# Two middle pairs of the second sweep: output products with the weights standing, turned, stored to scratch rows and added to the output by whole-chunk transfers

## The chip, the cores and the metric

The kernel runs on one core of one Trainium2 chip. The metric is the device time of one execution in microseconds (us). The engines are named as in the profile: PE is TensorE's matmul, PEld its weight load, DVE is VectorE, ACT is ScalarE, POOL is GpSimd and SP is SyncE, which here only issues DMAs.

## What is computed

Attention between 512 tokens and 32 state rows (8 batches, 8 heads of 64) gives 8 chunks of 544 rows by 512 columns. Two feed-forward blocks follow, over all 4352 rows. The second of them is the one that matters here:

```
x = relu(x @ w_in); x = (x * x) @ w_out            # 512 -> 2048 -> 512
a = x @ w1; b = x @ w2                              # 512 -> 1024, twice
h = (a * b) @ w3                                    # 1024 -> 1024
out = h @ w_out2                                    # 1024 -> 512
```

## The kernel before

The kernel first computes w34 = w3 @ w_out2 (1024 by 512), so that the last block is out = (a*b) @ w34. All products are done in float32 halves: each operand is split into a high and a low part (`split`: a cast on ACT, a difference on DVE), and each product is three matmuls (`PASSES`).

The last block makes two **sweeps** (`s`) over the rows. Sweep 0 takes the first 512 of the 1024 inner features, sweep 1 the others. The 512 token rows of the chunks are taken in **pairs** of chunks (the 32 state rows of all chunks are done apart, in `ab9` and `out9`): sweep 0 takes the pairs (3,4), (5,6), (7,2), (0,1), and sweep 1 the same backwards: (0,1) is its first pair, (7,2) and (5,6) are its middle pairs, (3,4) its last. For each pair:

- `quad` runs four times (m = 0 to 3) and makes a*b for 128 features at a time, with a scheme that needs seven products where eight blocks are multiplied. Its pieces (q0, q1) become the operands z of the next step (`to_z`, `late_z`).
- `out_pair` multiplies them by w34, again with seven products (`product`), and combines them into four blocks "11", "12", "21" and "22" (256 columns of one chunk each). `keep` copies a bank to SBUF, `put` adds a bank to what was kept.
- `make_pair` makes the operands of the next pair from what `load_pair` loads; its parts (`jobs`) are run by `do` between the products.

There are two forms of a product in `out_pair`. In the **straight** form z stands in the array and 256 columns of w34 move: 24 matmuls of 128x256 (line 1531), and rows of the bank are tokens. In the **turned** form w34 stands and 512 columns of z move: 12 matmuls of 128x512 (line 1520), and rows of the bank are output features. A turned block is kept, turned by DVE in 32x32 squares during the next pair's `quad`, and stored in runs of 256 bytes (`turn_out`: per block two transposes, two DMAs on SP's queue and two on POOL's). Before the change the first three pairs of sweep 0 are turned, and all of sweep 1 is straight.

Sweep 0 stores its results to `out`, except the halves of its first pair, which it stores to scratch (`o_scr`). In sweep 1 the first three pairs add theirs to `out` by accumulating DMAs of 256 KB on POOL's queue (line 1573, eight for a pair). The last pair (`ends`) loads sweep 0's halves back (`fetch`, on SP's queue), adds them on DVE and stores the sum.

Two loads of `out_pair` matter for the prediction. The products S3 and S4 take sums of weights from one slot of a tile, and `load_turn(s, 2)` overwrites S4's sum by S3's (two DMAs of 256 KB on SP's queue, line 1459) when the S4 product has read it; the S3 product is the sixth of the seven and can't start before they land. `fetch("12")` and `fetch("21")` are two DMAs of 256 KB each, ahead of them and behind them on the same queue.

Each engine runs its instructions in the order in which a scheduler has put them; `tc.issue_after` keeps one instruction behind another in that order.

Of the kernel before, what the change touches and what calls it, by code (L numbers as in the profile page):

```python
# [8 lines left out]
F32 = mybir.dt.float32  # L9
# [4 lines left out]
ALU = mybir.AluOpType  # L14
# [6 lines left out]
def kernel(  # L21
# [17 lines left out]
    nc = tc.nc  # L39
    B, H, S, D = x.shape  # L40
    NS = state.shape[2]
    DM = H * D
    DF = w_in.shape[1]
    D1 = w1.shape[1]
    T = S + NS
# [9 lines left out]
    NH = DM // 2  # L55
# [18 lines left out]
    dram = ctx.enter_context(tc.tile_pool(name="dram", bufs=1, space=DRAM))  # L74
# [1042 lines left out]
    NH = DM // 2  # L1117
# [193 lines left out]
    def quad(c0, c1, m, behind, in_order, behind_steps, early_jobs=()):  # L1311
        def product(*args, **kwargs):
            with tc.issue_after(left["quad"].ins) if in_order and "quad" in left else nullcontext():
                left["quad"] = product_of(*args, **kwargs)

        def product_of(ps, w, v, first=True, last=True):
            for kt in range(2):
                for k, (wi, vi) in enumerate(PASSES):
                    mm = nc.tensor.matmul(  # L1319
                        ps, W[w, kt][:, wi, m * P:(m + 1) * P], Y[v, kt][:, vi, :],  # L1320
                        start=(first and kt == 0 and k == 0), stop=(last and kt == 1 and k == 2),
                        skip_group_check=True,
                    )
            return mm

        def kept(i, ps):
            t = bp.tile([P, 512], F32, tag=f"s{i}", bufs=1 + (i == 0), name=f"s{i}")
            left["copy"] = nc.scalar.copy(t, ps)  # L1328
            return t

        def plus(t, ps):
            return nc.vector.tensor_tensor(out=t, in0=ps, in1=t, op=ALU.add)  # L1332

        A, D, E, C = bank_m("qa"), bank_y(m % 2, "qd"), bank_y(2, "qe"), bank_y(3, "qc")
        product(A, "A11", "B11", last=False)
        p1 = kept(0, A)
        with tc.issue_after(behind.ins) if behind else nullcontext():
            product(D, "S1", "T1", last=False)
        p5 = kept(1, D)
        with tc.issue_after(behind.ins) if behind else nullcontext():  # L1340
            product(E, "A12", "B21")
        plus(p1, E)
        product(A, "S2", "T2", first=False, last=False)
        u2 = kept(2, A)
        product(D, "S4", "B22", first=False)
        u2_sum = plus(u2, D)
        with tc.issue_after(u2_sum.ins), tc.issue_after(left["copy"].ins):
            for job in early_jobs:
                job()
        product(C, "A22", "T4")  # L1350
        product(A, "S3", "T3", first=False)
        u3 = kept(3, A)
        plus(p5, A)
        q1 = bp.tile([P, 512], F32, tag="qd" if m % 2 else "qb", bufs=1 if m % 2 else 2, name="q1")
        nc.vector.tensor_tensor(out=q1, in0=u2, in1=p5, op=ALU.mult)  # L1355
        if parts and m in behind_steps:
            add_behind(q1[:, :1])
        if m == 0:
            turn_out("11")
        turn_out("21" if m else "12")  # L1360
        plus(u3, C)
        if m % 2:
            q0 = bp.tile([P, 512], F32, tag="qc", bufs=2, name="q0")
        else:
            q0 = pa.tile([P, 512], F32, tag="r", bufs=2, name="q0")
        nc.vector.tensor_tensor(out=q0, in0=p1, in1=u3, op=ALU.mult)
        if m:
            turn_out("22")
        return to_z(m, q0, q1)
# [93 lines left out]
    TURNED = {"11": 5, "12": 6, "21": 2, "22": 4}  # L1463
    to_turn = {}

    def half_of(c, i, kept_back):
        if kept_back:
            o_scr[c, i] = dram.tile([S, NH], F32, name=f"oscr{c}_{i}")
            return o_scr[c, i]
        return out[c * T:c * T + S, i * NH:(i + 1) * NH]  # L1470

    def turn_out(block):
# [7 lines left out]
        for a in range(4):  # L1480
            (nc.gpsimd if a % 2 else nc.sync).dma_start(dst[a], o[a * NS:(a + 1) * NS].rearrange("p k d e -> p k (d e)"))

    TWO = ("s0", "yo", "r", "qb", "qc")

    def place(tag, name):
# [2 lines left out]

    def out_pair(c0, c1, s, jobs, last, first, more):
        ends = s == 1 and not more  # L1490
        turn = s == 0 and more
        jobs, gate, zcast = list(jobs), left["copy"], left["zcast"]
        mms = [left["quad"]]

        def do(n):
            with tc.issue_after(last.ins), tc.issue_after(gate.ins), tc.issue_after(zcast.ins):
                for job in jobs[:n]:
                    job()
            del jobs[:n]
# [8 lines left out]
            return w34_t[u][:, {"A11": 0, "A12": 2, "A22": 3}.get(w, 1)]  # L1508

        def product(*args, **kwargs):  # L1510
            with tc.issue_after(mms[-1].ins) if s == 0 else nullcontext():
                mms.append(product_of(*args, **kwargs))

        def product_of(ps, w, v, first=True, last=True):
# [33 lines left out]
        def keep(block, ps, tp0=0):  # L1548
            ts = []
            for tp, p in enumerate(ps, tp0):  # L1550
                if ends:
                    t = o_in.pop((block, tp))
                    nc.vector.tensor_tensor(out=t, in0=p, in1=t, op=ALU.add)
                else:
                    tag = "tp" if turn and AT[block][tp] == "s1" else AT[block][tp]
                    t = place(tag, "o")
                    nc.scalar.copy(t, p)
                ts.append(t)
            return ts

        def put(block, ts, ps, tp0=0):
            c, i = where(block)
            for tp, t in enumerate(ts, tp0):
                nc.vector.tensor_tensor(out=t, in0=ps[tp - tp0], in1=t, op=ALU.add)  # L1564
                if turn:
                    continue
                rows_t = "(p j) e -> p j e" if c < BLK else "(j p) e -> p j e"
                dst = out[c * T:c * T + S, i * NH:(i + 1) * NH].rearrange(rows_t, j=J)[:, 2 * tp:2 * tp + 2]
                src = t.rearrange("p (j e) -> p j e", j=2)
                if s == 0 or ends:  # L1570
                    nc.sync.dma_start(dst, src)
                else:
                    nc.gpsimd.dma_start(dst, src, accum_op=ALU.add)  # L1573
            if turn:
                to_turn[block] = half_of(c, i, first), ts

        for block in ("11", "22") if ends else ():
            fetch(block)
# [4 lines left out]
        bD = [bank_m("od") for _ in range(2)]  # L1583
        product(bD, "S1", "T1", last=False)
        t22 = keep("22", bD)
        do(1 if turn else 3 if more else 2)
        late(1)
        fetch("12")
        product(bD, "S4", "B22", first=False)
# [80 lines left out]
    for s, todo in enumerate((turns, turns[::-1])):  # L1670
# [16 lines left out]
        for i, (c0, c1) in enumerate(todo):  # L1687
            jobs = []
            for m in range(QM):
                early_jobs = []  # L1690
                if m == QM - 1 and s == 0 and i + 1 < len(todo):
                    jobs = make_pair(raw)
                    early_jobs, jobs = jobs[:2], jobs[2:]
                last = quad(c0, c1, m, after if i == 0 else None, s == 0 and (i > 0 or m > 0), (2,) if i else (0, 2), early_jobs)
                if m == 0 and i + 1 < len(todo):
                    raw = load_pair(*todo[i + 1])
                if m == 1 and i + 1 == len(todo) and s == 0:
                    raw = load_w(1)
# [41 lines left out]
```

## Time and profile before

| | |
|---|---|
| device time, median of 3 runs | 1198.16 us (1197.91 to 1198.72) |
| profiled execution | 1198.95 us, of which the span of the trace is 1196.7 us |
| PE busy | 1185.0 us, 99% of the span |
| DVE, ACT, POOL busy | 948.5, 694.5, 176.1 us |
| DMA | 179.22 MB |
| granted TensorE clock, mean | 0.998 |

The span runs from the first instruction to the end of the last one; some 2.2 us of the profiled execution lie outside it. A matmul's end is modelled, so the rate of PE is read from the starts of consecutive products, not from its busy time.

### The profile page before, as it was taken

The page shows a single profiled execution, that of the slowest core. Times are in us where ns is not written, and L with a number is a line of the kernel's source. Part 1 is how long each engine was busy: PE and PEld are TensorE (multiplying, and loading weights), DVE is VectorE, ACT ScalarE, POOL GpSimd, SP SyncE. Part 2 cuts the span into 40 slices and gives each one's busy share as a digit, 9 for nine tenths or more (in the row PEclk, how much of TensorE's full clock was granted, in tenths as well). Part 3 has the DMA queues.
Part 4 walks back from the last instruction along what each step waited for, and adds up shares of the span by engine and source line. Part 5 has one row for each costly group of instructions (what it writes and reads, how often), then busy time and mean ns, then how long its engine had stood idle before and what let it go on. Part 6 is the DMA issues. An engine that isn't in the chain of part 4 may idle for free.

```text
span 1196.7 us, 18436 instructions
## 1 busy us (share of the span) xinstructions
PE 1185.0 (99%) x6736; PEld 967.4 (81%) x6736; DVE 948.5 (79%) x1697; ACT 694.5 (58%) x1263; POOL 176.1 (15%) x249
## 2 busy tenths in 40 slices
PE   7999999999999999999999999999999999999998
PEld 5677777777777777777888888888888989898988
DVE  6989877778878674677778986989797958787877
ACT  6777556565656565777767663536454525353542
POOL 0000013323331200012231001020100001211210
PEclk9999999999999999999999999999999999999999
DMA  8675778946885933346696685673423631625334
GB/s 253 140 229 191 184 219 224 204 120 177 171 208 166 260 106 110 107 115 111 92 220 230 223 210 133 110 158 76 111 88 98 216 111 33 144 49 127 62 65 139
DMA packets 181876, 179.22 MB, mean 150 GB/s; under 512 B 103433, under 2 KB 134921, under 8 KB 181257
## 3 DMA queue, kind: packets, MB, share of 16 engines
q1 hardware_dynamic: 141128, 109.61, 31.6%
q0 software_dynamic: 38640, 65.03, 25.9%
q10 hardware_dynamic: 2016, 3.41, 0.8%
q8 instruction: 53, 0.87, 0.3%
q14 instruction: 39, 0.31, 0.1%
HBM read 114.43 MB, written 74.06 MB: 158 GB/s over the span
## 4 chain that ended last, share of the span: by engine, by line
PE 96%; DVE 2%; ACT 1%; DMA 1%; issue 0%; SPq 0%; DVEq 0%
PE y L594 22%; PE qa L1319 11%; PE qd L1319 7%; PE ps_w L1132 4%; PE qc L1319 4%; PE qe L1319 4%; PE oa L1531 3%; PE qa L966 3%; PE ps_sw L507 3%; PE od L1531 2%; PE oa L1520 2%; PE ab L1394 2%; PE qd L966 2%; PE y L566 1%; PE od L1520 1%; PE oe L1531 1%
## 5 line engine op out<-in xcount | busy, mean ns | idle before, releaser
L594 PE MATMUL y<-ghl,wo 128*128 128x512 f32 x1152 | 279.7, 392 | 0.1
L594 PEld LDWEIGHTS y<-ghl,wo 128*128 128x128 f32 x1152 | 214.5, 188 | 57.4 <-issue 12.6
L1328 ACT COPY s<-qa 128x512 f32<-128x512 f32 x96 | 56.5, 589 | 173.3 <-PE qa L1319 173.2
L1319 PE MATMUL qa<-yq,wq 128*128 128x512 f32 x576 | 143.3, 389 | 0.0
L538 DVE TENSOR_TENSOR ghl<-r,ghl 128x512 fp32r<-128x512 f32 (+1 forms) x112 | 72.6, 648 | 74.7 <-ACT ghl L537 65.2
L1319 PEld LDWEIGHTS qa<-yq,wq 128*128 128x128 f32 x576 | 107.9, 188 | 22.1
L1319 PE MATMUL qd<-yq,wq 128*128 128x512 f32 x384 | 97.4, 389 | 0.0
L1264 DVE TENSOR_TENSOR z<-q,z 128x512 fp32r<-128x512 f32 x112 | 73.7, 683 | 20.4 <-ACT z L1263 20.4
L1319 PEld LDWEIGHTS qd<-yq,wq 128*128 128x128 f32 x384 | 72.1, 188 | 15.0
L1263 ACT CAST z<-q 128x512 fp32r<-128x512 f32 x112 | 68.4, 625 | 23.2 <-DVE q L1355 5.6
L536 ACT ACTIVATE r<-r 128x512 f32<-128x512 f32 (+1 forms) x112 | 67.6, 604 | 4.2 <-DVE yo L605 1.4
L537 ACT CAST ghl<-r 128x512 fp32r<-128x512 f32 (+1 forms) x112 | 66.2, 591 | 2.8
L92 DVE TENSOR_TENSOR yq<-yraw,yq 128x512 fp32r<-128x512 f32 x98 | 64.1, 681 | 1.3 <-ACT yq L91 1.2
L1332 DVE TENSOR_TENSOR s<-qa,s 128x512 f32<-128x512 f32 x32 | 22.1, 690 | 53.6 <-ACT s L1328 53.6
L91 ACT CAST yq<-yraw 128x512 fp32r<-128x512 f32 x98 | 57.8, 625 | 7.0 <-DVE yraw L1240 5.0
L1573 POOL DMA_DIRECT2D out_dram<-o x24 | 28.8, 1585 | 207.2 <-DVE o L1564 207.2
L1319 PE MATMUL qe<-yq,wq 128*128 128x512 f32 x192 | 48.7, 389 | 0.0
L1319 PE MATMUL qc<-yq,wq 128*128 128x512 f32 x192 | 48.7, 389 | 0.0
L1132 PE MATMUL ps_w<-wo,w3T 128*128 128x512 f32 x192 | 44.2, 390 | 0.0
L1267 DVE TENSOR_TENSOR q<-q,q 128x512 f32<-128x512 f32 x64 | 43.0, 681 | 0.1
L1319 PEld LDWEIGHTS qe<-yq,wq 128*128 128x128 f32 x192 | 36.0, 188 | 7.5
L1319 PEld LDWEIGHTS qc<-yq,wq 128*128 128x128 f32 x192 | 36.0, 188 | 7.5
(724 smaller groups left out, 2516.8 us busy)
## 6 DMA issues: line engine op xcount, KB each, us to landing
yraw<-yscr SPq DMA_DIRECT2D x56, 256.0 KB, 5.4
raw<-in_moe_w_out_dram SPq DMA_DIRECT2D x16, 512.0 KB, 4.7
yscr<-yo SPq DMA_DIRECT2D x32, 256.0 KB, 3.5
raw<-in_moe_w_dram POOLq DMA_DIRECT2D x64, 128.0 KB, 3.7
raw<-in_moe_w_dram POOLq DMA_DIRECT2D x16, 512.0 KB, 7.0
raw<-in_moe_w_in_dram SPq DMA_DIRECT2D x12, 512.0 KB, 4.5
xb<-in_x_dram SPq DMA_DIRECT2D x96, 64.0 KB, 3.2
X<-in_x_dram SPq DMA_DIRECT2D x12, 512.0 KB, 8.3
```

The costliest lines, as they stand in the source:

```text
L91: nc.scalar.copy(hi, src)
L92: return nc.vector.tensor_tensor(out=lo, in0=src, in1=f32(hi), op=ALU.subtract)
L536: nc.scalar.activation(r[:, :n], r[:, :n], ACTF.Square)
L537: casts.append(nc.scalar.copy(t[:, HI, :n], r[:, :n]))
L538: done.append(nc.vector.tensor_tensor(out=t[:, LO, :n], in0=r[:, :n], in1=f32(t[:, HI, :n]), op=ALU.subtract))
L594: mm = nc.tensor.matmul(y_ps[c, d][:, :n], wo_t[f][:, wi, d * P:(d + 1) * P], t[:, gi, :n], start=(f == f0 and k == 0), stop=(f == f1 - 1 ...
L966: nc.tensor.matmul(ps[d], wt[:, wi, d * P:(d + 1) * P], v[:, kt, gi, :], start=(first and kt == 0 and k == 0), stop=(last and kt == 1 and ...
L1132: mm = nc.tensor.matmul(ps, t[:, wi, (j % 4) * P:(j % 4 + 1) * P], wo2_t[j][:, vi, :], start=(j == 0 and k == 0), stop=(j == N1 - 1 and k ...
L1263: left["cast"] = nc.scalar.copy(t[:, HI], q)
L1264: return nc.vector.tensor_tensor(out=t[:, LO], in0=q, in1=f32(t[:, HI]), op=ALU.subtract)
L1319: mm = nc.tensor.matmul(ps, W[w, kt][:, wi, m * P:(m + 1) * P], Y[v, kt][:, vi, :], start=(first and kt == 0 and k == 0), stop=(last and k ...
L1531: mm = nc.tensor.matmul(ps[tp][:, t % 2 * NH:(t % 2 + 1) * NH], Z[v, idx][:, vi, t * P:(t + 1) * P], straight(rhs[:, wi]), start=(first an ...
```

## The change

`out_pair` now runs the two middle pairs of sweep 1 in the turned form as well (`turn`). Their turned blocks are stored to a new scratch tensor for each chunk (`osum`, 512 rows of 512), in the next pair's `quad`, in the same way as in sweep 0. `add_turned` then adds each whole scratch chunk to `out` with one accumulating DMA of 1 MB from DRAM to DRAM on POOL's queue, in the form in which `add_behind` (line 230) already adds partial sums of an earlier stage. It is called with m = 3 of the next pair's `quad`, right behind q1; a copy of one column on POOL holds it there. For the second middle pair, the next pair is the last of the kernel.

The sixteen accumulating stores of these two pairs go. Moved besides: in the `quad` with m = 3 of the two middle pairs the first two jobs of the next pair's `make_pair` now run early, as they did in sweep 0; in every turned pair, sweep 0's too, the next job waits until the second kept bank of block "22" was copied; the products of the last two `quad`s and of the middle pairs are held in written order.

```diff
@@ quad
         nc.vector.tensor_tensor(out=q1, in0=u2, in1=p5, op=ALU.mult)
+        if to_add and m == QM - 1:
+            add_turned(q1[:, :1])
         if parts and m in behind_steps:
@@ half_of
-    def half_of(c, i, kept_back):
+    to_add = {}
+
+    def half_of(c, i, kept_back, s):
+        if s == 1:
+            if c not in to_add:
+                to_add[c] = dram.tile([S, DM], F32, name=f"osum{c}")
+            return to_add[c][:, i * NH:(i + 1) * NH]
         if kept_back:
@@ new
+    def add_turned(t):
+        gate = nc.gpsimd.tensor_copy(tick, t)
+        with tc.issue_after(gate.ins):
+            for c in sorted(to_add):
+                nc.gpsimd.dma_start(out[c * T:c * T + S, :], to_add.pop(c), accum_op=ALU.add, max_dma_last_dim=512)
+
@@ out_pair
         ends = s == 1 and not more
-        turn = s == 0 and more
+        turn = more and not (s == 1 and first)
...
-            with tc.issue_after(mms[-1].ins) if s == 0 else nullcontext():
+            with tc.issue_after(mms[-1].ins) if s == 0 or not first and more else nullcontext():
...
-                    nc.scalar.copy(t, p)
+                    left["kept"] = nc.scalar.copy(t, p)
...
-                to_turn[block] = half_of(c, i, first), ts
+                to_turn[block] = half_of(c, i, first, s), ts
...
-        do(1 if turn else 3 if more else 2)
+        with tc.issue_after(left["kept"].ins) if turn else nullcontext():
+            do(1 if turn else 3 if more else 2)
@@ the loop over pairs
-                if m == QM - 1 and s == 0 and i + 1 < len(todo):
+                if m == QM - 1 and i + 1 < len(todo) and not (s == 1 and i == 0):
...
-                last = quad(c0, c1, m, after if i == 0 else None, s == 0 and (i > 0 or m > 0), (2,) if i else (0, 2), early_jobs)
+                last = quad(c0, c1, m, after if i == 0 else None, i > 1 or s == 0 and (i > 0 or m > 0), (2,) if i else (0, 2), early_jobs)
```

Three places show what the change makes of the engines' orders. The first is PE in the second middle pair, whose seven products are, before (z stands; w34b and s, the weights, move; rows of three matmuls alternate between the two s where "..." stands):

```order
L1531 MATMUL oa<-w34b,z 128x256 x24
L1531 MATMUL od<-s_9758,z 128x256 x3
L1531 MATMUL od<-s_9761,z 128x256 x3
...
L1531 MATMUL od<-w34b,z 128x256 x24
L1531 MATMUL oe<-w34b,z 128x256 x24
L1531 MATMUL oa<-s_9758,z 128x256 x3
L1531 MATMUL oa<-s_9761,z 128x256 x3
...
L1531 MATMUL oa<-w34b,z 128x256 x24
L1531 MATMUL oc<-w34b,z 128x256 x24
```

Of the change:

```order
L1534 MATMUL oa<-z,w34b 128x512 x12
L1534 MATMUL od<-z,s_9758 128x512 x3
L1534 MATMUL od<-z,s_9761 128x512 x3
...
L1534 MATMUL od<-z,w34b 128x512 x12
L1534 MATMUL oe<-z,w34b 128x512 x12
L1534 MATMUL oa<-z,s_9758 128x512 x3
L1534 MATMUL oa<-z,s_9761 128x512 x3
...
L1534 MATMUL oa<-z,w34b 128x512 x12
L1534 MATMUL oc<-z,w34b 128x512 x12
```

The seven products keep their order, oa<-z,w34b near the end being S3; each is now twelve matmuls of 512 columns in place of 24 of 256.

The second is the end of POOL's queue, from the first accumulating store of sweep 1 on. The row of before is the one with -; the rows of the change, with +, begin behind the stores of the first pair and of the turned blocks of (7,2), whose scratch chunks are osum_10757 and osum_10724; osum_11235 and osum_11268 are those of (5,6).

```order
-L1573 DMA out_dram<-o 128x2x256 x24
...
+L1587 DMA out_dram<-o 128x2x256 x8
...
+L1492 COPY tick<-q_11128 128x1
+L1495 DMA out_dram<-osum_10757 2048x128
+L1495 DMA out_dram<-osum_10724 2048x128
+L1489 DMA osum_11235<-turned 32x16x64 x2
+L1489 DMA osum_11268<-turned 32x16x64 x2
+L1489 DMA osum_11235<-turned 32x16x64 x2
+L1489 DMA osum_11268<-turned 32x16x64 x2
+L1492 COPY tick<-q_11621 128x1
+L1495 DMA out_dram<-osum_11235 2048x128
+L1495 DMA out_dram<-osum_11268 2048x128
```

Two whole-chunk additions now stand at the head of the second middle pair's products, and two at the head of the last pair's, with nothing of POOL's behind them. SP's order of the last pair's products is the one of before: `fetch("12")`, the two loads of S3's sum, two stores, `fetch("21")`, six stores.

The third is ACT at the start of the third pair of sweep 0, where the od copies are the kept banks of block "22". Before:

```order
L1557 COPY o<-oa 128x512 [waits PE_49]
L91 CAST yq<-yraw 128x512 [waits DVE_49]
L1263 CAST z<-q_8774 128x512 [waits DVE_49,Activation_49]
L91 CAST yq<-yraw 128x512
L1263 CAST z<-q_8777 128x512 [waits DVE_49,Activation_49]
L1557 COPY o<-od 128x512 [waits PE_49] x2
```

Of the change:

```order
L1571 COPY o<-oa 128x512 [waits PE_49]
L91 CAST yq<-yraw 128x512 [waits DMAHW2_49]
L1263 CAST z<-q_8774 128x512 [waits DVE_49,Activation_49]
L91 CAST yq<-yraw 128x512 [waits DMAHW3_49]
L1263 CAST z<-q_8777 128x512 [waits DVE_49,Activation_49]
L1571 COPY o<-od 128x512 [waits PE_49] x2
```

Another job's casts (of B21, which wait for their load) have taken the place of the job that was moved behind the copies (T1): two casts of the next pair stand ahead of the od copies as before.

## Rows read from the trace of the kernel before

**Rows 1.** The page: span, busy time by engine, the chain that ended last.

```profile
span 1196.7 us, 18436 instructions
...
PE 1185.0 (99%) x6736; PEld 967.4 (81%) x6736; DVE 948.5 (79%) x1697; ACT 694.5 (58%) x1263; POOL 176.1 (15%) x249
...
PE 96%; DVE 2%; ACT 1%; DMA 1%; issue 0%; SPq 0%; DVEq 0%
```

**Rows 2.** Timeline of PE, 690 to 1200: start, us, instructions, [idle before].

```profile
807.01 2.88 PE L1520 MATMUL oa<-z,w 128*128 128x512 f32 x12
...
820.76 2.88 PE L1520 MATMUL oa<-z,w 128*128 128x512 f32 x12
...
826.20 1.52 PE L1319 MATMUL qa<-yq,wq 128*128 128x512 f32 x6
...
870.41 3.04 PE L1520 MATMUL od<-z,w 128*128 128x512 f32 x12 [0.45 <-ACT o L1557]
```

**Rows 3.** Timeline of PE, 1050 to 1200.

```profile
1055.44 3.02 PE L1531 MATMUL oa<-w34b,z 128*128 128x256 f32 x24
...
1075.43 1.53 PE L1319 MATMUL qa<-yq,wq 128*128 128x512 f32 x6
...
1171.59 3.02 PE L1531 MATMUL oa<-w34b,z 128*128 128x256 f32 x24
...
1187.11 3.08 PE L1531 MATMUL oa<-w34b,z 128*128 128x256 f32 x24
```

**Rows 4.** Windows: stretch, length, busy us by engine, PE clock, DMA share, GB/s.

```profile
749.77:768.93 19.16, 19.16 (x85) 15.69 (x84) 19.16 (x33) 13.41 (x25) 2.01 (x2) 1.00 0.63 94
...
826.20:864.28 38.08, 38.08 (x169) 31.54 (x168) 31.30 (x52) 14.74 (x26) 5.18 (x8) 1.00 0.42 112
864.28:884.16 19.88, 19.43 (x85) 15.62 (x84) 19.87 (x34) 14.34 (x26) 0.00 (x0) 1.00 0.16 53
...
1075.43:1113.52 38.09, 38.09 (x171) 31.54 (x170) 27.31 (x45) 14.12 (x25) 5.87 (x5) 1.00 0.49 110
```

**Rows 5.** Line 1459, window 1182 to 1183: S3's sum in the last pair.

```profile
L1459 SPq DMA_DIRECT2D w34b<-w34u x2: 338/360/382, 1182.1 to 1182.5; - x2
...
DMA to landing us min/median/max: 4.6/4.8/4.9
```

**Rows 6.** The page, costliest groups: the accumulating stores.

```profile
L1573 POOL DMA_DIRECT2D out_dram<-o x24 | 28.8, 1585 | 207.2 <-DVE o L1564 207.2
```

**Rows 7.** Line 1478, turned blocks' transposes: ns min/median/max, first and last start.

```profile
L1478 DVE STREAM_TRANSPOSE turned<-o x24: 668/701/705, 777.2 to 901.7; 128x512 f32<-128x512 f32 x24
```

**Rows 8.** Line 230, the 1 MB additions of an earlier stage.

```profile
L230 POOL DMA_DIRECT2D yscr<-yscr x5: 1808/1828/1894, 704.1 to 800.8; - x5
...
DMA to landing us min/median/max: 9.5/9.9/15.7
```

**Rows 9.** Windows of 2 us in one of these additions, issued at 744.7.

```profile
747.00:749.00 2.00, 2.00 (x10) 1.65 (x10) 1.97 (x4) 1.03 (x2) 0.00 (x0) 1.00 1.19 142
749.00:751.00 2.00, 2.00 (x11) 1.65 (x10) 2.00 (x4) 1.03 (x3) 0.00 (x0) 1.00 1.45 180
```

**Rows 10.** Timeline of DVE, 1160 to 1200: q1 with m = 3 of the last pair.

```profile
1173.61 0.68 DVE L1355 TENSOR_TENSOR q<-s,s 128x512 f32<-128x512 f32 x1
```

**Rows 11.** DMA issues, 1180.9 to 1181.7: fetch("12") of the last pair.

```profile
opart<-oscr SPq DMA_DIRECT2D x2, 256.0 KB, 3.0
```

**Rows 12.** The chain that ended last, 1000 to 1200: start, us, what.

```profile
1185.79 3.86 DMA opart<-oscr
```

**Rows 13.** Line 1459, window 814.5 to 816: S3's sum, nothing beside it.

```profile
L1459 SPq DMA_DIRECT2D w<-w34u x2: 337/337/337, 814.8 to 815.5; - x2
...
DMA to landing us min/median/max: 3.3/3.3/3.3
```

**Rows 14.** Line 1459, window 765 to 767: two such loads beside a 1 MB addition.

```profile
DMA to landing us min/median/max: 6.4/6.6/6.8
```

**Rows 15.** DMA issues, 706.6 to 708.95, beside an addition: KB each, us to landing.

```profile
s<-w34u SPq DMA_DIRECT2D x4, 256.0 KB, 10.1
```

## Prediction

> **What bounds the kernel now.** I read the page first: PE is busy 1185.0 of 1196.7 us, and the chain that ended last is 96% PE [rows 1]. So time is won only by making PE's own stream shorter, and lost by making PE wait, or by lengthening what follows PE at the end. Next I read the timeline of PE, for the rate of each form of an output product and for the few waits. Then the windows over whole pairs and whole quads, to see whether DVE, ACT and POOL have room for what the change gives them. Last I read the end of the trace, load by load, since the change puts new transfers there.
>
> The reader is to see three things. First, a straight pair takes 1075.43 - 1055.44 = 19.99 us from its first product to the next quad, and a turned pair takes 826.20 - 807.01 = 19.19 us [rows 2, 3]; the first turned pair takes 19.16 and the third 19.88, because there PE waits for a copy on ACT [rows 2, 4]. Second, a quad that carries turned transposes is as long as one that doesn't, 38.08 against 38.09 us, with DVE at 31.30 and 27.31 us of it [rows 4]. Third, in the last pair PE's S3 product starts at 1187.11 [rows 3], and the two loads that it needs are issued at 1182.1 and 1182.5 and take 4.6 and 4.9 us [rows 5]: they land at 1186.7 and 1187.4. The second half of the sum is first read 3 matmuls after the first, 3 x 0.119 = 0.36 us (a product of 24 is 19.99 / 7 = 2.86 us), at 1187.47. The loads have 0.4 us and 0.1 us to spare.
>
> **The change, part by part.**
>
> *Turned products in the two middle pairs.* The rows price this directly. The order of ACT and DVE in the changed middle pairs is that of the first two turned pairs of sweep 0, so I take 19.16 and 19.19 in place of 19.99 twice: 0.83 + 0.80 = 1.6 us gained. Bounds: two pairs like the third one, 19.88, gain 0.2; two pairs with no wait at all, seven products at 2.72 us (826.20 - 820.76 is two of them), 19.04 each, gain 1.9. Matmul for matmul, the trace has 227 ns for 512 columns and 119 for 256, so the smaller form pays some 11 ns more for every 512 columns. The Trainium skill speaks against so large a gain: its page "TensorE: Matmul & The Clock Gate", section "Back-to-back issue gap", gives N/2.4 + 2.5 ns for a warm gap, and by that estimate 24 gaps of 109.2 ns against 12 of 215.8 would gain 0.03 us a product, 0.4 us in fourteen. The trace disagrees, since both forms of the same product stand in it, and the measurement decides.
>
> *Waits in sweep 0.* The job that is held behind the od copies could take away the third pair's wait, 19.88 - 19.19 = 0.7 us [rows 2, 4]. But in the new order of ACT two other casts stand in its place ahead of the same copies. I take 0, and keep a gain of 0.7 as the far end.
>
> *Stores.* Sixteen of the 24 accumulating stores go. They sit on POOL, which waited 207.2 us for them in all [rows 6]; PE doesn't wait for POOL, so that gains nothing. In their place come 32 stores of turned blocks and 16 transposes, 16 x 0.70 = 11.2 us of DVE [rows 7]. They lie in the next quads, under PE: the quads of sweep 0 carry the same load, plus early jobs, at 31.30 of 38.08 us of DVE [rows 4]. Cost 0; without that cover it would be up to 5.6 us a pair. The early jobs move work out of the output products into the quad, as in sweep 0: 0.
>
> *The whole-chunk additions.* This is the part with a price. In the trace the same transfer (1 MB, DRAM to DRAM, accumulating, POOL's queue) takes POOL 1.83 us to issue and lands 9.5 to 15.7 us after [rows 8]; while it moves alone, 180 GB/s are moved [rows 9], so one occupies the DMA engines for 1.05 / 0.18 = 5.8 us and two for 11.7. In the last pair, POOL is released by q1, at 1173.61 + 0.68 = 1174.3 [rows 10]. Some 0.5 us for the copy, and the additions are issued at about 1174.8 and 1176.6. The lead until data moves is 9.5 - 5.8 = 3.7 us at most, some of it behind the data, so they move from about 1177.5 until 1189 at the earliest, with nothing else running. But from 1180.9 the last pair's own loads run: fetch("12"), two of 256 KB [rows 11], S3's sum, two more, and fetch("21") at 1185.79 [rows 12], with two stores between. That is the stretch with 0.1 us to spare.
>
> What a load of S3's kind pays beside such an addition, the trace shows twice. Two loads that meet one addition took 6.4 to 6.8 us, where two alone took 3.3 [rows 13, 14]. Four in a row that meet one (issued at 704.1, landed 15.7 us later [rows 8]) took 10.1 [rows 15]. The last pair has four in a row within 1.6 us, and two additions, so it is nearest to the row of four: I take 10.1. S3's sum then lands at 1182.1 + 10.1 = 1192.2 and 1182.5 + 10.1 = 1192.6, and S3 starts at 1192.2 instead of 1187.11, 5.1 us later; the second half is needed at 1192.56 and costs nothing more. Behind S3 on PE stand S3's other matmuls and the end of the last product, and behind them DVE's last sums and the stores. So the end moves by **5.1 us**. Bounds: 0 if the loads land as before; with 6.4 and 6.8 us they land at 1188.5 and 1189.3, 1.4 + 0.4 = 1.8 us. At the far end it is the other chain: fetch("21") was the last wait, 3.86 us until 1189.65 [rows 12], and with 10.1 us it lands at 1195.9, 6.2 late; I don't take that, since the additions are nearly over by then. The Trainium skill's page "DMA: Bandwidth & Descriptors", section "Queues, rings and completion order", says that each DMA engine takes turns between queues, packet by packet. An equal share would be an estimate of twice the time: 9.2 and 9.8 us in place of 4.6 and 4.9, landing at 1191.3 and 1192.3, 4.8 us late. Rows 13 and 14 agree with twice the time; the row of four is above it.
>
> In the second middle pair the first two additions meet S3's load too. A turned pair issues it 7.8 and 8.5 us behind its first product (814.8 and 815.5 against 807.01) and starts S3 13.75 us behind it (820.76) [rows 2, 13]. The additions are released at about +2.7, as in the last pair (1174.3 against 1171.6 [rows 3]), and run well past +15. Two loads beside an addition, 6.4 and 6.8 us, land at +14.2 and +15.3; S3 starts 0.4 late, and its second half, needed 3 x 0.227 = 0.7 us later, is late by another 0.4 to 0.5: **0.9 us**. Bounds: 0 with 3.3 us, 4.1 with the 10.1 of rows 15.
>
> **The sum:** -1.6 + 0.9 + 5.1 = +4.4 us. Against the profiled execution, 1198.95 us (a span of 1196.7), that is 1203.3; that execution lies 0.8 above the median of the runs, 1198.16, so against the median it is **1202.6 us**. A difference under 0.2%, 2.4 us, can hardly be told from none here.
>
> **The rivals.**
>
> *The loads are squeezed less.* The additions started 6 us ahead of S3's loads, and two loads beside one took 6.4 to 6.8 [rows 14]. Then -1.6 + 0.9 + 1.8 = +1.1: 1199.3 us, no difference. Against it stands that fetch("12") goes ahead on the same queue.
>
> *The additions hide* (the other side). Their place is the same, their price 0: the loads of the last pair land as before, because the additions are mostly over by 1182 or give way to SP's queue. Then -1.6: 1196.5 us; with the third pair's wait gone as well and the best rate, -1.9 - 0.7 = -2.6: 1195.6. It decides where S3's loads land within 5.0 us. For it speaks only that an addition alone lands after 9.5 us [rows 8], the first one at 1184.3; against it, that the second stands behind the first, and that every load which met an addition in the trace was at least twice as long [rows 14, 15].
>
> *The second middle pair waits longer.* Two additions at once could give its S3 load the 10.1 us too, 4.1 in place of 0.9: +7.6, 1205.8 us. Against it: only two loads run there.
>
> *The turned form brings nothing*, because of new waits on ACT like that of the third pair: a gain of 0.2 in place of 1.6, 1204.0 us, inside the forecast's case.
>
> **How the numbers follow.** Forecast: 0.56, with its own range of 1200.6 to 1204.2 (the end late by 3.5 to 6, the middle pair by 0 to 1.5). Squeezed less: 0.20. Hidden: 0.14, of which 0.06 with everything gained. Longer wait in the middle pair or at the end: 0.10. The range from 1196.4 (the hidden case) to 1205.0 leaves out less than 2 in 10. Slower by over 0.2%: 0.56 + 0.10 = 0.66. Within 0.2%: 0.20 + 0.08 = 0.28. Faster: 0.06.
>
> **What would show it.** In the profile after: line 1534 with 12 matmuls of 512 columns in sweep 1, and the first middle pair at 19.2 us (19.9 would refute the gain). In the second middle pair an idle PE of about 0.9 us ahead of S3, released by a DMA. At the end four additions of line 1495, the last two landing at 1190 or later; S3's loads at about 10 us; an idle PE of about 5 us ahead of S3; fetch("21") landing near 1194. The quads stay at 38.1. If S3's loads land within 5 us in the last pair, the prediction is wrong and the kernel is faster or the same; if the quads are longer, DVE's cover was not there.

## The result and the profile after

The changed kernel takes 1205.26 us (median; 1204.02 to 1206.11), against 1198.04 for the kernel before in the same rounds: a ratio of 1.0059, 95% interval 1.0046 to 1.0072, or 7.1 us slower. The prediction was 1202.6, slower, with a range of 1196.4 to 1205.0: the direction was right, and the time lies 0.3 us above the range. The profiled execution took 1205.78 us.

The page of the changed kernel (span, busy time, chain that ended last):

```profile
span 1204.0 us, 18175 instructions
...
PE 1186.2 (99%) x6568; PEld 960.0 (80%) x6568; DVE 958.3 (80%) x1713; ACT 693.9 (58%) x1263; POOL 176.0 (15%) x255
...
PE 94%; DMA 3%; DVE 1%; SPq 1%; ACT 1%; issue 0%; DVEq 0%; ACTq 0%
```

Against [rows 1], the span is 7.3 us longer and PE is busy for only 1.2 us more: most of what was added is time in which PE does nothing. DMA's share of the chain went from 1% to 3%.

Timeline of PE in the changed kernel, 1050 to 1205, at the starts of pairs and quads and at the waits:

```profile
1055.57 2.88 PE L1534 MATMUL oa<-z,w34b 128*128 128x512 f32 x12
...
1074.74 1.52 PE L1319 MATMUL qa<-yq,wq 128*128 128x512 f32 x6
...
1112.83 2.88 PE L1534 MATMUL oa<-z,w34b 128*128 128x512 f32 x12
...
1127.59 3.40 PE L1534 MATMUL oa<-z,w34b 128*128 128x512 f32 x12 [0.90 <-DMA w34b<-w34u]
...
1133.55 1.52 PE L1319 MATMUL qa<-yq,wq 128*128 128x512 f32 x6
...
1171.63 3.02 PE L1545 MATMUL oa<-w34b,z 128*128 128x256 f32 x24
...
1190.66 0.59 PE L1545 MATMUL oa<-w34b,z 128*128 128x256 f32 x3 [3.35 <-DMA w34b<-w34u]
1191.72 4.28 PE L1545 MATMUL oa<-w34b,z 128*128 128x256 f32 x21 [0.46 <-DMA w34b<-w34u]
1195.83 1.95 PE L1645 MATMUL oc<-w34b,z 128*128 128x256 f32 x15
```

Three readings. The first middle pair takes 1074.74 - 1055.57 = 19.17 us. The second takes 1133.55 - 1112.83 = 20.72 us, with a wait for S3's loads in it. And the last pair starts at 1171.63, where it started at 1171.59 before [rows 3]: by then the gain of the turned form is spent. From there to the end of the span it is 32.4 us, where it was 1196.7 - 1171.59 = 25.1. So the whole net loss lies in the last pair.

Windows of the changed kernel (columns as in [rows 4]): first middle pair, the quads behind both middle pairs, the second middle pair, PE's idle stretch in the last pair, and the 21 matmuls behind it:

```profile
1055.57:1074.74 19.17, 19.17 (x85) 15.69 (x84) 19.17 (x33) 13.41 (x25) 0.00 (x0) 1.00 0.17 55
1074.74:1112.83 38.09, 38.09 (x170) 31.54 (x169) 31.86 (x53) 14.69 (x26) 5.22 (x8) 1.00 0.42 111
1112.83:1133.55 20.72, 19.71 (x85) 15.53 (x84) 19.15 (x33) 14.12 (x26) 4.35 (x3) 1.00 0.93 134
1133.55:1171.63 38.08, 38.08 (x169) 31.53 (x168) 31.00 (x51) 14.21 (x25) 5.23 (x8) 1.00 0.37 87
...
1187.16:1190.66 3.50, 0.16 (x2) 0.03 (x1) 1.86 (x3) 0.00 (x0) 0.00 (x0) 1.00 1.22 275
1191.72:1195.83 4.11, 4.11 (x21) 4.11 (x22) 0.69 (x1) 0.00 (x0) 0.00 (x0) 0.58 1.26 244
```

The quads with transposes are as long as before, with DVE at 31.0 to 31.9 us of 38.1. The last row is new: behind PE's wait the granted clock is 0.58, and 21 matmuls that take 21 x 0.119 = 2.5 us take 4.11. That 0.58 is a mean of the two levels, 1.2 and 2.4 GHz; a window inside the stretch has the lower one alone:

```profile
1192.25:1195.25 3.00, 3.00 (x16) 3.00 (x16) 0.69 (x1) 0.00 (x0) 0.00 (x0) 0.50 1.26 245
```

The four whole-chunk additions of the changed kernel, line 1495:

```profile
L1495 POOL DMA_DIRECT2D out_dram<-osum x4: 1877/2272/2682, 1116.7 to 1176.5; - x4
...
DMA to landing us min/median/max: 10.5/16.0/22.4
```

S3's loads in the second middle pair and in the last pair, line 1461 in the windows 1115 to 1125 and 1180 to 1185:

```profile
L1461 SPq DMA_DIRECT2D w34b<-w34u x2: 338/338/338, 1120.6 to 1121.3; - x2
...
DMA to landing us min/median/max: 6.9/7.1/7.3
```

```profile
L1461 SPq DMA_DIRECT2D w34b<-w34u x2: 337/347/357, 1182.1 to 1182.6; - x2
...
DMA to landing us min/median/max: 8.4/8.8/9.1
```

The last addition is issued at 1176.5 and lands 22.4 us later, at 1198.9. One by itself took 9.5 to 9.9 us [rows 8]; this one also stands behind another, and what that alone costs is read below, from the run with the additions earlier. S3's loads of the last pair are issued when they were before and take 8.4 to 9.1 us for 4.6 to 4.9 [rows 5].

The end of the chain that ended last, of the changed kernel (start, us, what):

```profile
1185.83 10.79 DMA opart<-oscr
1196.64 0.69 DVE opart L1567
1197.33 0.60 DVE opart L1578
1197.93 0.66 DVE opart L1567
```

The load of `fetch("21")` starts when it did before and takes 10.79 us for 3.86 [rows 12]. It lands at 1196.62, 7.0 us later than before; the end is 7.3 us later.

### The profile page after: what moved, and what is told of

It is laid out like the page before. It is cut to its first block, busy times and chain, and to the rows that moved or that the text cites. A ratio compares the mean times of both kernels' runs of the same rounds, so it can differ in the third digit from the quotient of the medians.

```text
span 1204.0 us, 18175 instructions
## 1 busy us (share of the span) xinstructions
PE 1186.2 (99%) x6568; PEld 960.0 (80%) x6568; DVE 958.3 (80%) x1713; ACT 693.9 (58%) x1263; POOL 176.0 (15%) x255
## 4 chain that ended last, share of the span: by engine, by line
PE 94%; DMA 3%; DVE 1%; SPq 1%; ACT 1%; issue 0%; DVEq 0%; ACTq 0%
PE y L594 21%; PE qa L1319 11%; PE qd L1319 7%; PE ps_w L1132 4%; PE qc L1319 4%; PE qe L1319 4%; PE oa L1534 3%; PE qa L966 3%; PE ps_sw L507 3%; PE od L1534 2%; PE ab L1396 2%; PE qd L966 2%; PE oa L1545 2%; PE od L1545 1%; PE y L566 1%; PE oc L1534 1%
## 5 line engine op out<-in xcount | busy, mean ns | idle before, releaser
L1132 PEld LDWEIGHTS ps_w<-wo,w3T 128*128 128x128 f32 x192 | 35.8, 188 | 7.5
```

What stands on the lines that cost most here:

```text
L1132: mm = nc.tensor.matmul(ps, t[:, wi, (j % 4) * P:(j % 4 + 1) * P], wo2_t[j][:, vi, :], start=(j == 0 and k == 0), stop=(j == N1 - 1 and k ...
```

## The experiments

Ratios are to the kernel before, run on the same chip in the same rounds (medians 1198.2 to 1198.5 us), with 95% intervals. Each edit is to the changed kernel.

**No additions.** The four additions are left out, so `out` lacks them; the stores of the turned blocks stay.

```diff
-                nc.gpsimd.dma_start(out[c * T:c * T + S, :], to_add.pop(c), accum_op=ALU.add, max_dma_last_dim=512)
+                to_add.pop(c)
```

> Leaves out the four whole-chunk additions, so the sweep-1 part of two pairs never reaches the output; everything else of the change is kept. Theory A (the additions collide with loads on SP's queue, all else of the change is hidden or a gain): PE waits for no load, both middle pairs take 19.2 us, the end is as before: 1198.0 - 1.6 = 1196.4 us. Rival B (the turned form or the moved jobs cost something by themselves: transposes, 256-byte stores, held orders): still slower than before, 1200 us or more. S3's loads in the last pair: A 4.6 to 4.9 us, as before.

Measured: 1195.96 us, ratio 0.9979 (0.9969 to 0.9989). Timeline of PE, the last pair's first product and S3 in it:

```profile
1169.31 3.02 PE L1545 MATMUL oa<-w34b,z 128*128 128x256 f32 x24
...
1184.85 3.02 PE L1545 MATMUL oa<-w34b,z 128*128 128x256 f32 x24
```

S3 starts 15.54 us behind the pair's first product, as before (1187.11 - 1171.59 = 15.52), and PE waits for no load. So the additions are the whole loss, and what is left without them is a gain of 2.5 us, 1.3 to 3.7 by the interval: the 1.6 of the turned form lies in it. The other 0.9 is taken up under "the kernel before again".

**No last additions.** Only the two additions of the last pair are left out.

```diff
 def add_turned(t):
+        if 5 in to_add:
+            to_add.clear()
+            return
```

> Leaves out the last two additions only, those that run in the last pair; the two in the second middle pair are kept. Theory A: the end is as before the change, the second middle pair keeps its wait for S3's load (20.7 us in place of 19.2): 1198.0 - 0.8 + 0.7 = 1197.9 us, same as before. Rival B: no different from the change, 1205 us. If the two places add up, this run lies 1.5 us above the run with no additions.

Measured: 1196.94 us, ratio 0.9988 (0.9979 to 0.9997). S3 of the second middle pair still waits (timeline of PE):

```profile
1127.43 3.40 PE L1537 MATMUL oa<-z,w34b 128*128 128x512 f32 x12 [0.33 <-DMA w34b<-w34u]
```

So the last two additions cost (1.0059 - 0.9988) x 1198 = 8.5 us and the first two (0.9988 - 0.9979) x 1198 = 1.1 us, the latter no larger than its uncertainty. The parts, -2.5 + 1.1 + 8.5, add up to the measured 7.1 by the way they are formed.

**Last two as plain copies.** The last two transfers move the same megabytes without adding, so that sweep 0's part of those chunks is overwritten.

```diff
+                if c in (5, 6):
+                    nc.gpsimd.dma_start(out[c * T:c * T + S, :], to_add.pop(c), max_dma_last_dim=512)
+                    continue
```

> The last two transfers copy the scratch chunks over the output in place of adding to it (so 1024 rows lack sweep 0's part); same bytes of scratch, same queue, same moment. Theory A1 (what hurts is the accumulation, which reads the destination too and holds the DMA engines 5.8 us for 1 MB): a plain copy moves 1 MB in about 3 us, both are nearly over when fetch(12) is issued; S3's loads take about 5 to 6 us and the end is late by 0 to 1.5 us: 1198 to 1199.5 us. Rival A2 (any 2 MB on POOL's queue at that moment do the same): fetch(21) takes 9 us or more, 1203 to 1205 us.

Measured: 1198.88 us, ratio 1.0003 (0.9994 to 1.0012). The two copies, line 1496 in the window 1170 to 1180:

```profile
L1496 POOL DMA_DIRECT2D out_dram<-osum x2: 1043/1048/1053, 1175.4 to 1176.4; - x2
...
DMA to landing us min/median/max: 6.8/8.1/9.4
```

They land 6.8 and 9.4 us after their issue, where the additions took 10.5 and 22.4, and S3's loads take 5.9 to 6.1 us: theory A1's numbers. The copies cost (1.0003 - 0.9988) x 1198 = 1.8 us, the additions 8.5: four fifths of the harm go away when the additions become copies. But the edit changed more than the summing. POOL's queue of DMA packets (packets, MB, share of 16 engines), window 1174 to 1200, of the changed kernel and of this one:

```profile
q0 software_dynamic: 4128, 2.10, 65.1%
...
q0 software_dynamic: 544, 2.10, 25.7%
```

The additions go in 4128 packets of some 510 bytes, the copies of the same 2.10 MB in 544 of some 3900. No run has these additions in large packets or these copies in small ones, so whether the summing or the small packets do the harm stays open.

**One last addition.** Of the last two, only chunk 5's is made; chunk 6 lacks sweep 1's part.

```diff
+                if c == 6:
+                    to_add.pop(c)
+                    continue
```

> In the last pair only one of the two whole-chunk additions is made (that of chunk 5; the addition of chunk 6 is left out, so its rows lack sweep 1's part). Theory: what holds the end up is the traffic of two additions one behind the other; one alone is issued at about 1175.4, lands 10 to 11 us later (1186), and S3's loads meet only its end: 5.5 to 7 us instead of 8.4 to 9.1, fetch of block 21 4 to 5 us instead of 10.8, the end 0.5 to 2.5 us late instead of 7.2: 1197.5 to 1200.5 us. Rival: the price is one of meeting an accumulating transfer at all, whichever it is, so that half of the loss or more stays: 1201.5 us or more. Second rival: each addition costs its half of the 8.5 us that the two cost together: 1201.0 to 1201.5.

Measured: 1198.56 us, ratio 1.0004 (0.9996 to 1.0013). S3's loads in the window 1170 to 1190 of this kernel:

```profile
L1461 SPq DMA_DIRECT2D w34b<-w34u x2: 338/348/358, 1182.3 to 1182.8; - x2
...
DMA to landing us min/median/max: 5.6/5.8/6.0
```

The first theory's numbers hold for S3's loads and for the time. One addition costs (1.0004 - 0.9988) x 1198 = 1.9 us, the second, queued behind it, another 6.6: the harm is in the queue of two reaching past S3's loads and over `fetch("21")`.

**No `fetch("21")`.** The two loads of block 21's first halves are left out, with a copy on DVE in place of the sum that reads them; block 21 of the last pair lacks sweep 0's part.

```diff
-            for tp in range(2) if ends else ():
+            for tp in range(2) if ends and block != "21" else ():
...
+                if ends and block == "21":
+                    t = place(AT[block][tp], "opart")
+                    nc.vector.tensor_copy(t, p)
-                if ends:
+                elif ends:
```

> The changed kernel with the two loads of block 21's first halves in the last pair left out (fetch of 21), and a copy on the vector engine in the place of the sum that reads them, so that this block of the last pair lacks sweep 0's part. Theory: the end is set by that load, which took 10.8 us, while the products' own chain, held up 3.4 us by S3's loads and slowed by the lower clock behind that wait, ends some 1.2 to 1.5 us earlier: 1203.4 to 1204.3 us, with S3's start still 3 to 4 us late. Rival: both chains end together, and nothing changes: 1204.8 to 1205.7. Second rival: the load's own 0.5 MB is a part of the crowd that delays S3's sum; without it S3 starts within 1 us of its time and the end comes back by 4 us or more: 1201 or less.

Measured: 1203.17 us, ratio 1.0042 (1.0030 to 1.0054), a little below the first theory's numbers. Its chain that ended last:

```profile
1180.89 9.07 DMA w34b<-w34u
1190.00 4.29 PE oa L1545 x21
1194.31 0.69 DVE opart L1581
```

S3's loads take as long as with `fetch("21")` and hold PE up as long (3.8 us in all), so that load is not what crowds them. The last pair starts at 1169.95 here and the span ends at 1200.8, 30.85 us for 32.37 in the changed kernel and 25.11 before. So of the 7.3 us at the end, 5.7 come through S3's chain alone, and 1.5 more through `fetch("21")` (2.0 by the two ratios).

**Additions earlier.** The computation is complete; the additions are released behind p1 with m = 2 in place of q1 with m = 3.

```diff
         plus(p1, E)
+        if to_add and m == 2:
+            add_turned(p1[:, :1])
...
-        if to_add and m == QM - 1:
-            add_turned(q1[:, :1])
```

> Complete computation. The same four additions, released earlier: behind p1 of the quad with m = 2 (about 18 us earlier) in place of q1 with m = 3. Theory A: in the second middle pair they run from about 1098 to 1114 and in the last pair from about 1157 to 1172, under products that load nothing; S3's loads take 3.3 and 4.9 us again, no wait is left and the gain of the turned form shows: 1196.4 us (1196.0 to 1197.0). Rival B: additions or transposes cost wherever they stand, 1200 us or more. Rival D: they now meet the turned stores or the fetches of 11 and 22 and make PE wait there: 1197.5 to 1200 us.

Measured: 1196.43 us, ratio 0.9984 (0.9975 to 0.9992): 1.9 us faster than the kernel before. The additions, line 1495:

```profile
L1495 POOL DMA_DIRECT2D out_dram<-osum x4: 1880/2272/2679, 1099.2 to 1157.6; - x4
...
DMA to landing us min/median/max: 10.1/12.6/16.5
```

The last is issued at 1157.6, 19 us earlier than in the changed kernel, and has landed at 1174.1; S3's loads of the last pair take 4.7 to 4.8 us and PE waits for none. The first two of these additions, line 1495 in the window 1098 to 1104, have no other transfer of data beside them:

```profile
L1495 POOL DMA_DIRECT2D out_dram<-osum x2: 1880/2280/2679, 1099.2 to 1100.3; - x2
...
DMA to landing us min/median/max: 10.3/12.6/14.9
```

So two additions in a row take 1100.3 + 14.9 - 1099.2 = 16.0 us from the first issue to the last landing with nothing beside them. At the end of the changed kernel, issued from 1175.4 on, they would have been over at 1191.4; the other 7.5 us, until 1198.9, came with the loads and stores beside them. The same four transfers, moved to where no load is urgent, cost nothing that these runs can tell.

**Straight form, the moves kept.** The middle pairs are straight again, with accumulating stores and no additions; early jobs and held order stay.

```diff
-        turn = more and not (s == 1 and first)
+        turn = s == 0 and more
```

> The two middle pairs of sweep 1 go back to the straight form with accumulating stores, so that there are neither turned blocks nor whole-chunk additions; the early jobs, the held order of the products and the job behind the kept bank stay as in the changed kernel. Theory: the moves are worth nothing, the turned form gains 1.6 us and the additions lose the rest. Then this kernel is as long as the one before, ratio 0.9995 to 1.0005, a middle pair takes 19.9 to 20.0 us from its first product to the next quad, and S3's loads of the last pair take 4.6 to 5.0 us. Rival: without the additions the changed kernel was 2.5 us faster than the one before where the turned form should give 1.6, so the moves bring the other 0.9 us: ratio 0.9992. Second rival: the early jobs make the quads longer, ratio 1.001 or more.

Measured: 1206.12 us, ratio 1.0061 (1.0049 to 1.0073). The first theory and the first rival are refuted. The second rival's numbers hold (1.001 or more, longer quads), though they say little of the size; its cause, the early jobs, is only a part, as the next runs show. Timeline of PE behind the first middle pair, and the window over three starts there:

```profile
1075.68 1.55 PE L1319 MATMUL qa<-yq,wq 128*128 128x512 f32 x6
1077.07 1.52 PE L1319 MATMUL qd<-yq,wq 128*128 128x512 f32 x6
1080.95 2.06 PE L1319 MATMUL qe<-yq,wq 128*128 128x512 f32 x6 [2.36 <-DVE o L1578]
```

```profile
1075.68:1118.08 42.40, 40.04 (x170) 32.60 (x169) 26.51 (x44) 14.01 (x25) 6.30 (x6) 0.96 0.47 101
...
1080.95:1085.37 4.42, 4.42 (x12) 3.47 (x13) 1.24 (x2) 0.00 (x0) 3.61 (x3) 0.62 1.00 219
```

PE waits 2.36 us for the pair's last sums on DVE and then runs twelve matmuls at a granted clock of 0.62. Both quads behind middle pairs are 42.3 to 42.4 us long in place of 38.1, 8.6 us in all. This is not the kernel before plus the moves: the straight form runs three jobs behind the kept bank where the turned form runs one (`do(1 if turn else 3 ...)`), so that with two early ones five jobs stand ahead of the sums. Three runs take that apart; each has this edit too, and the one shown.

**Straight, one job behind the bank.**

```diff
-            do(1 if turn else 3 if more else 2)
+            do(1 if turn or s == 1 and more and not first else 3 if more else 2)
```

> The straight form with the moves kept was 7.9 us slower than the kernel before: its quads behind the middle pairs took 42.4 us in place of 38.1, because PE waited there for the last sums of the output products on the vector engine (2.4 us) and then ran at a lower granted clock. Here one more thing is set as in the turned form: one job, not three, runs behind the kept bank of block 22. Theory: three jobs there on top of the two early ones are what pushes the sums back on the vector engine; with one the wait is gone, the quads take 38.1 us, and the kernel is as long as before, ratio 0.9995 to 1.0010. Rival: the held order of the products is the cause, and this changes nothing: ratio 1.005 or more.

Measured: 1198.15 us, ratio 0.9999 (0.9990 to 1.0008). The product that waited, in the timeline of PE, has no wait left:

```profile
1078.20 1.52 PE L1319 MATMUL qe<-yq,wq 128*128 128x512 f32 x6
```

The first theory holds. With the jobs at the turned form's pace, all the moves together are worth nothing that stands clear of the noise.

**Straight, free order,** and **straight, no early jobs,** with three jobs behind the bank:

```diff
-            with tc.issue_after(mms[-1].ins) if s == 0 or not first and more else nullcontext():
+            with tc.issue_after(mms[-1].ins) if s == 0 else nullcontext():
...
-                last = quad(c0, c1, m, after if i == 0 else None, i > 1 or s == 0 and (i > 0 or m > 0), (2,) if i else (0, 2), early_jobs)
+                last = quad(c0, c1, m, after if i == 0 else None, s == 0 and (i > 0 or m > 0), (2,) if i else (0, 2), early_jobs)
```

> The straight form with the early jobs (and three jobs behind the kept bank), but with the products of the middle pairs and of the last two pairs' quads free to be reordered, as in the kernel before. Theory of the jobs' pace: the sums are as late on the vector engine as in the straight form with all moves, but PE has other products to put ahead of the one that waits, as it did in the kernel before: half the loss or less, ratio 1.000 to 1.003. Rival, the held order alone is the cause: ratio 0.9995 to 1.0005, with the sums as early as before. Second rival, the order makes no difference: 1.005 or more.

```diff
-                if m == QM - 1 and i + 1 < len(todo) and not (s == 1 and i == 0):
+                if m == QM - 1 and s == 0 and i + 1 < len(todo):
```

> The straight form in held order, without the two early jobs: three jobs behind the kept bank of block 22, as in the kernel before. Theory of the jobs' pace: the sums come as early as in the kernel before, within 1 us; the product that waited 2.4 us waits 0 to 0.6, and the ratio is 0.9995 to 1.0015. Rival, the held order is the cause by itself: ratio 1.005 or more.

Measured: 1198.57 us, ratio 1.0005 (0.9996 to 1.0015), and 1197.45 us, ratio 0.9995 (0.9986 to 1.0005). Each mends the loss by itself. In the first, the last sums on DVE are as late (the second sum of S3's bank starts 1078.46 - 1071.67 = 6.8 us behind the oc product, and 1079.61 - 1072.82 = 6.8 with all moves), but PE has another product to put in front. In the timelines: the second sum of S3's bank on DVE with free order, the same sum with all moves, and two of PE's products with free order, a qa product ahead of the qe product that waited:

```profile
1078.46 0.69 DVE L1578 TENSOR_TENSOR o<-oa,o 128x512 f32<-128x512 f32 x1
...
1079.61 0.69 DVE L1578 TENSOR_TENSOR o<-oa,o 128x512 f32<-128x512 f32 x1
...
1077.27 1.52 PE L1319 MATMUL qa<-yq,wq 128*128 128x512 f32 x6
...
1080.35 1.52 PE L1319 MATMUL qe<-yq,wq 128*128 128x512 f32 x6
```

So the loss needs both: late sums, and an order that can't step around them.

**Turned, no early jobs:** the last edit alone, with turned form and additions as in the change.

> The changed kernel (turned form, additions) without the two early jobs in the quads of the middle pairs. Theory: the early jobs cost and bring nothing by themselves, as the prediction has it: 1204.8 to 1206.0, with quads of 38.1 us and the same waits. Rival: the turned form needs them; without them two more jobs stand between its products, with one job less behind block 22 than the straight form has, and the last sums come late: quads of 39 to 42 us and 1206.5 to 1212.

Measured: 1208.59 us, ratio 1.0086 (1.0069 to 1.0102): the rival's time. The interval still touches that of the changed kernel (1.0046 to 1.0072), so the 3.3 us between the medians are not far from the noise. Windows of it, the quad behind the first middle pair, the second middle pair, and the quad behind that:

```profile
1076.65:1115.63 38.98, 38.66 (x169) 31.40 (x168) 32.63 (x53) 14.63 (x26) 5.22 (x8) 1.00 0.42 108
1115.63:1137.23 21.60, 20.45 (x86) 15.39 (x84) 19.51 (x32) 14.13 (x26) 4.27 (x3) 1.00 0.93 143
1137.23:1175.61 38.38, 38.37 (x170) 31.47 (x169) 32.15 (x53) 14.91 (x26) 5.24 (x8) 1.00 0.36 78
```

They are 0.9, 0.9 and 0.3 us longer than in the changed kernel (the quads a little short of the rival's 39 to 42 us); its last pair is 0.6 longer. Another 1.9 us of this one execution lie ahead of the first middle pair and were there before the quad that the edit touches. With one job behind the bank, the two early ones seem not to be free extras; that they carry what no longer fits between the products is not shown.

**The kernel before again.**

> The kernel before, once more, for a profile of the same chip. Theory: the 0.9 us by which the changed kernel without its additions was faster than the sum said lie at the end: the last stores of the kernel before land as late here as in its first profile, 9.6 us from the start of S3 to the end of the span, against 8.75 without the additions. Rival: they are a matter of the chip, and the kernel before ends 8.7 to 8.9 us behind S3's start here too.

Measured: 1198.77 us. Its span ends 9.3 us behind S3's start, between the two theories; the four straight kernels without additions above end 9.8, 9.4, 9.0 and 8.9 us behind it with the same work there. So the end scatters by some 0.9 us between these executions, and the 0.9 us that the kernel without additions gained beyond 1.6 needs no cause in the change; none was shown.

## Why the prediction was right in sign and short in size

**What bounds it, and the turned form.** Right. The first middle pair took 19.17 us for 19.16, and the second would have taken 19.3 without its waits: 20.72 less the 0.90 ahead of S3 and the 3.40 - 2.88 = 0.52 between S3's halves. The third pair of sweep 0 kept its wait of 0.45 us for ACT, as taken. The formula that the prediction set against the gain says less than it was taken for: the Trainium skill's page "TensorE: Matmul & The Clock Gate", section "Back-to-back issue gap", gives it for an isolated matmul. In this stream, where a weight load goes with each matmul (6568 of each in the page of the profile), the trace has 227 and 119 ns.

**Stores and early jobs.** Right at 0 for all the moves together: the quads stayed at 38.1 us, and the run with one job behind the bank measures the moves at 0.9999. What the text gave as the reason ("as in sweep 0") left out that this holds at the turned form's pace of jobs only.

**The second middle pair.** Right in kind, short in size: 1.5 us for 0.9. The loads took 6.9 to 7.3 us where the row of one addition gave 6.4 to 6.8. The wait is not a fixed number: with the same two additions the profile of the kernel without the last two shows 0.33 us ahead of S3, that with plain copies 1.86.

**The end.** This is the step that failed, and the sum with it: 5.1 us were taken and 7.3 came. The prediction had the far end in hand, `fetch("21")` with 10.1 us landing at 1195.9, and set it aside "since the additions are nearly over by then". They were not: the second one lands at 1198.9. The text took 1189 "at the earliest" as their end, and was short in two ways. Two additions by themselves take 16.0 us from the first issue, which makes it 1191.4; and the transfers beside them hold the additions up as the additions hold the loads up, by another 7.5 us, where the text gave the delay to one side only. The rows had this: the 15.7 us of [rows 8] belong to the addition that met the loads of [rows 15], against 9.5 to 9.9 alone. `fetch("21")` took 10.79 us, and the run without it shows what that decides: 1.5 us.

Inside S3's chain two errors all but cancelled. S3's loads took 8.4 to 9.1 us, not the 10.1 of rows 15, so S3 started 3.55 us late, not 5.1. But its second half was waited for as well (0.46 us), and then PE ran at a granted clock of 0.58, which cost another 4.11 - 2.5 = 1.6 us that no term foresaw: 5.6, close to the 5.7 that the run without `fetch("21")` shows. The Trainium skill's page "DMA: Bandwidth & Descriptors", section "Queues, rings and completion order", has each DMA engine take turns between queues; the prediction's estimate from it, an equal share, was 9.2 and 9.8 us for these loads. The measured 8.4 to 9.1 is a little less, and `fetch("21")`, at 2.8 times its time before, is well above twice.

Of the 2.7 us that the sum fell short, 0.6 lie in the second middle pair, 0.6 in S3's chain (5.7 for 5.1, close by luck of the two errors) and 1.5 in `fetch("21")`. With what was measured the sum is -1.6 + 1.5 + 7.3 = 7.2 us, against 7.1 between the medians and 7.3 between the spans. Of the rivals, "squeezed less" is close to what one addition alone does (ratio 1.0004), and "the additions hide" is what happens when they are released 19 us earlier (0.9984). "The second middle pair waits longer" gave 1205.8 us, close to the measured 1205.26, by luck: that pair waited 1.5 us, not 4.1, and the time was lost at the end.

## What to carry to other kernels

An accumulating transfer that no engine waits for can still cost the loads that run beside it: find the first loads that the bottleneck will wait for, and release the large transfer so that it has landed by then, its time taken longer than when it runs alone, and that of a second one behind it longer again. When two transfers share the DMA engines, delay both in the estimate, and follow every load to the end of the trace, not only the one that is waited for first. A part of a change that is undone alone may meet settings that were chosen for the other part, such as the number of jobs between two products; undo it with those settings.

## What the runs showed of the hardware that was not expected

- An accumulating 1 MB transfer from DRAM to DRAM took 10.5 us to land and the one queued behind it 22.4 us, beside loads; with nothing beside them 10.3 and 14.9 us. Plain copies of the same chunks, beside the same loads, took 6.8 and 9.4 us; they went in 544 packets where the additions took 4128.
- TensorE's granted clock fell behind an idle stretch, after PE had gone on: to 0.50, the level of 1.2 GHz, from 1192.25 to 1195.25, behind 3.35 and 0.46 us of idle (a mean of 0.58 over 21 matmuls), and to a mean of 0.62 over twelve matmuls behind 2.36 us. The kernel without `fetch("21")` shows the same 0.58 behind 3.30 and 0.45 us. Behind waits of 0.90 us, and of 1.86 us in the kernel with plain copies, it stayed at 1.00. Where the clock fell, the matmuls took 4.11 - 2.5 = 1.6 and 4.42 - 12 x 0.227 = 1.7 us longer.
